# Backward filling products behind the dV/dK products, issued as four 32-column tiles

## The chip, the core and the metric

The kernel runs on one core of a Trainium2 chip. A core has a matrix engine (PE; its weight loads are listed apart as PEld), a vector engine (DVE), an activation engine (ACT), a general engine (POOL) and a sync engine (SP) that issues most transfers. Each takes its own instructions in order, and they wait for one another by semaphores. The metric is the device time of one launch in microseconds (us), as the median of several runs. Before the change it is 1469.26 us (six runs, 1463.87 to 1473.15).

## The reference

A transformer block's forward pass and all its gradients, in bf16, for one sequence of S = 2048 rows of D = 448, H = 16 heads of 28 columns, and a feed-forward width of F = 1792:

```python
def _A_ref(x, wqkv, wo):
    qkv = transpose((x @ wqkv).reshape(B, S, 3, H, Dh), 2, 0, 3, 1, 4)
    q, k, v = qkv[0], qkv[1], qkv[2]
    p = softmax(einsum("bhqd,bhkd->bhqk", q, k) * Dh ** -0.5)
    o = einsum("bhqk,bhkd->bhqd", p, v)
    return transpose(o, 0, 2, 1, 3).reshape(B, S, D) @ wo
...
def _B_ref(x, w_gate, w_up, w_down):
    return (silu(x @ w_gate) * (x @ w_up)) @ w_down
...
xn = layernorm(x)
out = x + _A_ref(xn, wqkv, wo) + _B_ref(xn, w_gate, w_up, w_down)
# returned: out, and the gradients of x, wqkv, wo, w_gate, w_up, w_down for a given grad_out
```

## The kernel before, in words

The first part, up to about 640 us, is the forward attention with the feed-forward layer and its gradients filled in between. The second part is the backward attention, and the change lies there. Its loop goes over `NB` = 512 steps k: 4 groups of heads, 2 halves of a group, 4 chunks of 512 keys, 4 chunks of 512 queries, and 4 tiles of 128 queries. A step handles two heads, each held in 32 partitions or columns (`HP` = 32).

What a step issues is written out by hand, by m = k % 4 (the loop over `range(NB + 12)`):

- Every step begins with `row(k)`: four products with a contraction over 32 rows, two for the scores of step k (line 810, into `sb`) and two for the gradient of the probabilities of step k - 1 (line 818, into `db`). `sb` and `db` have three one-bank PSUM buffers each. They run in the array mode that the profile writes as 32*128: rows by columns of one tile.
- `ew(k)` then gives ACT the two exponentials that read `sb` (line 837) and DVE the two multiplications that read `db` and the exponentials of the step before (line 845).
- `kv` follows for steps whose inputs are due: four products (lines 918 and 922), which add to dV and dK of two heads. Each fills 32 of the 128 output columns of the array, so the four lie side by side: mode 128*32. At m = 1 and m = 2 usually two steps' worth is issued. After each 16 steps the sum is moved out of PSUM by ACT, and the next `kv` waits for m = 3 instead of m = 2.
- At m = 0 stands a transposition of dS (`tr_unit`, line 900, mode 128*128, also into a `db` buffer), at m = 1 the dQ products (`dq_unit`, line 949, 16 in mode 128*32, into the only `genb` bank, which ACT reads out in lines 953 and 962).
- The rest of PE's time goes to filling units, taken from the list `stream`: generators that yield after every product with its estimated duration. `fill_step(room)` runs products until the room is used up. The room is 400 ns (`R0`) before the transposition at m = 0 and without limit behind it, 250 (`R2`) at m = 2, and 750 (`R3`) at m = 3. With products of 189 ns each that is two and then the rest at m = 0, one at m = 2, four at m = 3.

The filling units, all in mode 128*128 (or 128*64 where a chunk has only 64 columns) and all into `genb`: the late columns of the feed-forward weight gradients (`late_dw`, line 884), the gradient of wqkv (`dwq_unit`, line 1014), the forward output (`y_unit`, line 1076), and two parts of the gradient of x (`dx_unit`, line 1132, and `dc_unit`, line 1176). Units of transpositions (`dsq_unit` line 982, `dsp_unit` line 1001) are in the list too; the change does not touch them.

So at m = 2 PE goes through row (32*128), kv (128*32), fill (128*128), and at m = 3 through row (32*128), fill (128*128), with kv in between only in the one case of four named above.

Of the kernel before, what the change touches and what calls it, by code (L numbers as in the profile page):

```python
# [17 lines left out]
D = 448  # L18
# [3 lines left out]
G = 4  # L22
HP = 32
NT = S // 128
NFC = F // 128
P = 128
# [77 lines left out]
def kernel(  # L104
# [23 lines left out]
    PE, DVE, ACTE, POOL, SP = nc.tensor, nc.vector, nc.scalar, nc.gpsimd, nc.sync  # L128
# [18 lines left out]
    xn_sp = xn_t[:, :NT * D].rearrange("p (t d) -> p t d", d=D)  # L147
# [399 lines left out]
    for i in range(len(chain) + LEAD):  # L547
# [4 lines left out]
        k = i - LEAD  # L552
# [115 lines left out]
    for c in range(3):  # L668
        k = 4 * c
        t = 4 * c + 4  # L670
# [99 lines left out]
    def have(*keys):  # L770
        for x in [x for x in slow if x[1] in keys]:
            slow.remove(x)
            SP.dma_start(out=x[2], in_=x[3])
# [19 lines left out]
    def store(o, i):  # L793
        held.append((now + 2, o, i))
        flush(0 if now < NB else 10 ** 9)
# [64 lines left out]
    k = n = 0  # L860
# [14 lines left out]
    fT = bk.tile([P, 4, 2, 4, P], BF16, name="dsp", bufs=1)  # L875
# [3 lines left out]
    def late_dw(c):  # L879
        d0, dn = DCH[c]  # L880
        have(("f",))
        ps = ps_g.tile([P, 2, P], FP32, name="genb")
        for t in range(NT):
            PE.matmul(ps[:dn], lhsT=xn_sp[:, t, d0:d0 + dn], rhs=fT[:, t // 4, :, t % 4, :],
                      start=(t == 0), stop=(t == NT - 1))
            if t < NT - 1:
                yield 110
        DVE.tensor_copy(out=w2[:dn, c], in_=ps[:dn])
        for a, o in enumerate((out_4, out_5)):
            store(o[d0:d0 + dn, F - P:], w2[:dn, c, a])  # L890
        yield 110

    dq_acc = bk.tile([P, S // 2], FP32, name="dq_acc", bufs=1)

    def tr_unit(b):
        ds = dss.pop(4 * b + 3)
        for qi in (3,) if b < NB // 4 - 1 else (2, 3):
            ps = ps_b.tile([P, 8, P], BF16, name="db", bufs=3)
            for c in range(8):
                PE.transpose(ps[:, c, :], ds[:, qi % 2, c // 4, (c % 4) * P:(c % 4 + 1) * P], ident_bf[:])  # L900
            o = dsT[b][:, qi].rearrange("p j kt s -> p (j kt) s")
            if qi == 2:
                DVE.tensor_copy(out=o, in_=ps[:])
            else:
                ACTE.copy(out=o, in_=ps[:])  # L905
# [84 lines left out]
    dsp = {}  # L990
# [19 lines left out]
    def dwq_unit(g, c, tag="genb"):  # L1010
        d0, dn = DCH[c]
        ps = (ps_b if tag == "rest" else ps_g).tile([P, 3 * P], FP32, name=tag, bufs=2 if tag == "rest" else 1)
        for t in range(NT):
            PE.matmul(ps[:dn, :], lhsT=xn_sp[:, t, d0:d0 + dn], rhs=dsp[g][:, t].rearrange("p k r -> p (k r)"),
                      start=(t == 0), stop=(t == NT - 1))
            if t < NT - 1:
                yield 162
        o = bk.tile([P, 3, 4, DH], BF16, name="dwq_o")
        p4 = ps[:].rearrange("p (k h r) -> p k h r", k=3, r=HP)
        cp = ACTE.copy if tag == "rest" else DVE.tensor_copy  # L1020
        cp(out=o[:dn, 0], in_=p4[:dn, 0, :, :DH])
        cp(out=o[:dn, 1:3, 0:2, :], in_=p4[:dn, 1, :, :DH].rearrange("p (k h) r -> p k h r", k=2))
        cp(out=o[:dn, 2, 2:4, :], in_=p4[:dn, 2, 0:2, :DH])
        cp(out=o[:dn, 1, 2:4, :], in_=p4[:dn, 2, 2:4, :DH])
        store(wq_out[d0:d0 + dn, :, g * 4 * DH:(g + 1) * 4 * DH],
              o[:dn].rearrange("p k h r -> p k (h r)"))
        s_done.add((g, c))
        yield 162
# [4 lines left out]
    NH = NFC // 2  # L1033
    ych, yts = {}, {}
# [16 lines left out]
    wd_sb = yp.tile([P, NFC, D], BF16, name="wd_sb", bufs=1)  # L1051
    wo_sb = yp.tile([P, G, D], BF16, name="wo_sb", bufs=1)
# [11 lines left out]
    def y_unit(ch, half, ti):  # L1064
        if ti == 0:
            have(("y", ch, half))
            nxt = 2 * ch + half + 2
            if nxt < 8:
                load_y(nxt // 2, nxt % 2)
        tsl = slice(ti * P, (ti + 1) * P)  # L1070
        mm = [(ych[ch, half][:, i, tsl], wd_sb[:, half * NH + i, :]) for i in range(NH)]
        if half:
            mm += [(ych[ch, 3][:, i, tsl], wo_sb[:, i, :]) for i in range(G)]
        ps = ps_g.tile([P, 512], FP32, name="genb")
        for i, (l, r) in enumerate(mm):
            PE.matmul(ps[:, :D], lhsT=l, rhs=r, start=(i == 0), stop=(i == len(mm) - 1))
            if i < len(mm) - 1:
                yield 189
        if half == 0:
            yts[ti] = yp.tile([P, D], FP32, name="yt", bufs=5)  # L1080
            DVE.tensor_tensor(out=yts[ti][:], in0=ps[:, :D], in1=ych[ch, 2][:, ti, :], op=ALU.add)
        else:
            y = yp.tile([P, D], BF16, name="y")
            DVE.tensor_tensor(out=y[:], in0=ps[:, :D], in1=yts[ti][:], op=ALU.add)  # L1084
            store(out0_d[:, 4 * ch + ti, :], y[:])
        yield 189


    dxs = {}
# [30 lines left out]
    def dx_unit(ch, fq, ti):  # L1120
        if ti == 0:
            have(("dx", ch, fq))
            nxt = 4 * fq + ch + 1
            if nxt < 12:
                load_dx(nxt % 4, nxt // 4)
        d = dxs[ch, fq]
        f0, f1 = FQ[fq]
        n = 2 * (f1 - f0)
        tsl = slice(ti * P, (ti + 1) * P)
        ps = ps_g.tile([P, 512], FP32, name="genb")  # L1130
        for i in range(n):
            PE.matmul(ps[:, :D], lhsT=d[:, i // 2, i % 2, tsl], rhs=dxs["w", fq][:, i // 2, i % 2, :],  # L1132
                      start=(i == 0), stop=(i == n - 1))
            if i < n - 1:
                yield 189
        o = dxs["g"][:, 4 * ch + ti, :]
        if fq == 0:
            ACTE.copy(out=o, in_=ps[:, :D])
        else:
            DVE.tensor_tensor(out=o, in0=ps[:, :D], in1=o, op=ALU.add)  # L1140
        yield 189
# [3 lines left out]
    dcs, dy2 = {}, {}  # L1145
# [23 lines left out]
    def dc_unit(t):  # L1169
        if t % 4 == 0:  # L1170
            have(("dc", t // 4))
            if t < 12:
                load_dc(t // 4 + 1)
        ps = ps_g.tile([P, 512], FP32, name="genb")
        for i in range(3 * G - 3):
            PE.matmul(ps[:, :D], lhsT=dcs[t // 4][:, i, (t % 4) * P:(t % 4 + 1) * P], rhs=dxs["wq"][:, i, :],
                      start=(i == 0), stop=(i == 3 * G - 4))
            if i < 3 * G - 4:
                yield 189
        DVE.tensor_tensor(out=dxs["g"][:, t, :], in0=ps[:, :D], in1=dxs["g"][:, t, :], op=ALU.add)  # L1180
        yield 189
# [14 lines left out]
    for t in range(NT):  # L1196
        stream.append((189 * 9, lambda t=t: dc_unit(t)))
# [25 lines left out]
    def fill_step(room):  # L1223
        nonlocal cur
        if cur is None:
            return
        for ns in cur:
            room -= ns
            if room < ns / 2:
                return  # L1230
        cur = None
# [3 lines left out]
    for k in range(NB + 12):  # L1235
        now = k
        if k < NB:
            g, hp, kc, qc, qi = steps[k]
            if hp == 1 and kc > 0 and qc == 2 and qi == 2 and g + 1 < G:
                load_k(g + 1, kc - 1)  # L1240
            if g > 0 and hp == 0 and kc == 0 and qc == 2 and qi == 2:
                load_k(g, 3)
            if hp == 1 and g + 1 < G and qi == 3 and (kc, qc) in NEXT:
                load_q(g + 1, NEXT.index((kc, qc)))
        m = k % 4
        if k <= NB:
            if k >= K0:
                row(k)
                ew(k)
            flush(k)  # L1250
            if 2 <= k:
                drop()
        if m:
            while kv_n < NB and kv_n <= k - (2 if m == 2 or kv_n % 16 == 15 else 3) and (m != 2 or kv_n % 16):
                kv(kv_n)
                kv_n += 1
        if m == 0:
            b = (k - 8) // 4
            if 9 <= k < NB and cur is None:
                fill_open(600)  # L1260
            fill_step(R0)
            if 0 <= b < NB // 4:
                tr_unit(b)
            fill_step(BIG)
        elif m == 1:
            b = (k - 13) // 4
            if 0 <= b < NB // 4:
                dq_unit(b)
        elif m == 2:
            if 9 <= k < NB:  # L1270
                fill_open(BIG)
                fill_step(R2)
        else:
            fill_step(R3)
    while stream:
        for _ in stream.pop(0)[1]():
            pass
# [14 lines left out]
    g = G - 1  # L1292
# [96 lines left out]
```

The softmax here doesn't subtract the row's maximum and nothing guards it: scores larger than these inputs give would overflow.

## Time and profile before

| | |
|---|---|
| median of six runs | 1469.26 us |
| the profiled execution's own time | 1473.15 us |
| its span, first to last instruction | 1471.4 us |
| mean granted clock of the matrix engine | 0.978 of full speed |
| PE / ACT / DVE busy, of the span | 91% / 86% / 78% |
| matmuls, weight loads | 12647, 12708 |

A row of the profile's list of groups gives the line, the engine, the operation, what it writes and reads, the shapes and the count, then the busy time in us, the mean duration of one in ns, the idle time of the engine just before it, and what ended that idle time. The groups of the backward loop on PE, ACT and DVE that matter here:

```profile
L845 DVE TENSOR_TENSOR ds_sb<-db,e_sb 128x512 bf16<-128x512 f32 x1024 | 648.2, 684 | 72.5 <-PE db L818 25.2
L837 ACT ACTIVATE e_sb<-sb 128x512 bf16<-128x512 f32 x1024 | 554.3, 611 | 60.4 <-PE db L818 43.7
L922 PE MATMUL acc<-ds_sb,qd 128*32 128x512 bf16 x1024 | 162.4, 394 | 0.0
L1132 PE MATMUL genb<-wguT,dau_c 128*128 128x448 bf16 x448 | 117.5, 356 | 6.3 <-ACT dq_st L962 3.8
L949 PE MATMUL genb<-dsT,kd 128*32 128x256 bf16 x2048 | 82.1, 282 | 5.9 <-DVE y L1084 4.3
```

The first says: 1024 multiplications on DVE, 648.2 us in all, 684 ns each; DVE sat idle for 72.5 us before them, 25.2 of which ended with a `db` product of line 818. [...]matmuls which follow one another overlap; how fast they pass is seen in the distance of their starts.

### The profile page before, as it was taken

How to read it: one execution, taken by the hardware profiler on the slowest of the kernel's cores; microseconds unless marked ns; L12 is line 12 of the kernel's file. 1: busy time of each engine (PE TensorE's matmuls, PEld its weight loads, DVE VectorE, ACT ScalarE, POOL GpSimd, SP SyncE). 2: the span in 40 equal slices, each digit the busy share in tenths (PEclk: the TensorE clock that was granted, in tenths of full speed). 3: DMA queues.
4: the chain of work that ended last, by engine and by line, in shares of the span. 5: the costliest groups of instructions: out<-in, count | busy, mean ns of one | idle time of the engine just before them, and what ended most of it. 6: DMA issues, size and time to landing. Idle time of an engine off the chain costs nothing. (4 is left out here: it accounts for less than half of the span.)

```text
span 1471.4 us, 34341 instructions
## 1 busy us (share of the span) xinstructions
PE 1338.5 (91%) x12647; PEld 544.0 (37%) x12708; DVE 1153.4 (78%) x1997; ACT 1263.4 (86%) x2193; POOL 363.3 (25%) x486
## 2 busy tenths in 40 slices
PE   5899999989999999888999989999999999899996
PEld 2333333333333333333333334433343444343343
DVE  6677656756667767487888879888889999899988
ACT  5798888988999988687888879899889899888974
POOL 6465424553344444000001101001001011010005
PEclk9999999999999999999899999999999999999998
DMA  5797957796788675699999999999999999999971
GB/s 150 166 203 194 206 116 183 155 206 154 155 171 190 142 179 139 200 198 194 210 200 201 212 206 189 202 210 209 220 196 187 198 216 201 209 205 199 201 141 59
DMA packets 697665, 271.14 MB, mean 184 GB/s; under 512 B 616129, under 2 KB 672153, under 8 KB 697497
## 3 DMA queue, kind: packets, MB, share of 16 engines
q1 hardware_dynamic: 692520, 262.82, 86.8%
q0 software_dynamic: 3568, 5.83, 1.9%
q8 instruction: 100, 1.64, 0.5%
q14 instruction: 69, 0.56, 0.1%
q10 hardware_dynamic: 1408, 0.30, 0.1%
HBM read 65.04 MB, written 59.90 MB: 85 GB/s over the span
## 5 line engine op out<-in xcount | busy, mean ns | idle before, releaser
L845 DVE TENSOR_TENSOR ds_sb<-db,e_sb 128x512 bf16<-128x512 f32 x1024 | 648.2, 684 | 72.5 <-PE db L818 25.2
L837 ACT ACTIVATE e_sb<-sb 128x512 bf16<-128x512 f32 x1024 | 554.3, 611 | 60.4 <-PE db L818 43.7
L611 ACT ACTIVATE eT<-s_w 128x1024 bf16<-128x1024 f32 x256 | 263.5, 1029 | 48.2 <-PE s_ps L608 45.4
L613 ACT ACTIVATE eT<-s_ps 128x512 bf16<-128x512 f32 x512 | 280.4, 612 | 0.0
L818 PE MATMUL db<-kd,qd 32*128 32x512 bf16 x1024 | 240.4, 386 | 20.6 <-DVE ds_sb L845 19.6
L810 PE MATMUL sb<-kd,qd 32*128 32x512 bf16 x1024 | 212.0, 390 | 8.0 <-DMA qd<-QD_d 4.3
L964 POOL TENSOR_TENSOR dq_acc<-dq_acc,dq_st 128x256 f32<-128x256 f32 x64 | 46.4, 725 | 587.3 <-ACT dq_st L962 587.3
L922 PE MATMUL acc<-ds_sb,qd 128*32 128x512 bf16 x1024 | 162.4, 394 | 0.0
L918 PE MATMUL acc<-e_sb,qd 128*32 128x512 bf16 x1024 | 160.5, 394 | 1.4 <-DVE dw_o L527 1.4
L905 ACT COPY dsT<-db 128x1024 bf16<-128x1024 bf16 x128 | 130.1, 1016 | 35.3 <-PE db L900 34.7
L379 POOL TENSOR_TENSOR nn<-nn,ag 128x512 f32<-128x512 f32 x56 | 71.2, 1271 | 250.7 <-DVE ag L377 242.1
L608 PE MATMUL s_ps<-QQ,KK 32*128 32x512 bf16 x512 | 125.5, 385 | 3.8
L1132 PE MATMUL genb<-wguT,dau_c 128*128 128x448 bf16 x448 | 117.5, 356 | 6.3 <-ACT dq_st L962 3.8
L608 PE MATMUL s_w<-QQ,KK 32*128 32x512 bf16 x512 | 100.3, 387 | 13.1 <-ACT eT L611 10.5
L810 PEld LDWEIGHTS <-qd 32*128 32x128 bf16 x1024 | 48.4, 91 | 152.5 <-issue 140.6
L420 PE MATMUL gen<-xn_t,f_sp 128*128 128x448 bf16 x416 | 91.8, 354 | 2.6 <-DVE nn L394 1.7
L949 PE MATMUL genb<-dsT,kd 128*32 128x256 bf16 x2048 | 82.1, 282 | 5.9 <-DVE y L1084 4.3
L420 PEld LDWEIGHTS <-f_sp 128*128 128x128 bf16 x640 | 55.7, 98 | 76.8 <-issue 31.9
L900 PE MATMUL db<-ident_bf,ds_sb 128*128 128x128 bf16 x1032 | 81.1, 223 | 1.1 <-DVE ds_sb L845 1.1
L900 PEld LDWEIGHTS <-ds_sb 128*128 128x128 bf16 x1032 | 69.5, 100 | 28.5 <-issue 9.7
L380 POOL TENSOR_TENSOR nn<-nn,tt 128x512 f32<-128x512 f32 x56 | 72.0, 1286 | 4.4
L450 PE MATMUL gen<-eT,VS 128*32 128x512 bf16 x1024 | 68.3, 383 | 4.5 <-DVE nn L394 2.4
(163 smaller groups left out, 1871.8 us busy)
## 6 DMA issues: line engine op xcount, KB each, us to landing
F_d<-hda SPq DMA_DIRECT2D x56, 384.0 KB
dau_c<-F_d SPq DMA_DIRECT2D x56, 256.0 KB
h_c<-F_d SPq DMA_DIRECT2D x24, 256.0 KB
qd<-QD_d SPq DMA_DIRECT2D x24, 256.0 KB
dc<-dqkvT_d SPq DMA_DIRECT2D x12, 384.0 KB
dsT<-ds_sb SPq DMA_TRANSPOSE x255
wT_d<-wT_f SPq DMA_DIRECT2D x14, 256.0 KB
KD_d<-qk_sp SPq DMA_DIRECT2D x7, 512.0 KB
```

Source lines behind the costliest of these rows:

```text
L420: PE.matmul(ps[:, :D], lhsT=fsp[fc][:, t // 4, w, t % 4, :], rhs=rhs[:, t, :], start=(t == 0), stop=(t == NT - 1))
L608: PE.matmul(sp4[hh], lhsT=KK[g][r:r + HP, kt * P:(kt + 1) * P], rhs=QQ[g][r:r + HP, qsl], start=True, stop=True, tile_position=(r, 0))
L611: ACTE.activation(out=e2[0][:], in_=wide[:], func=ACT.Exp, scale=SCALE)
L613: ACTE.activation(out=e2[1][:, j], in_=sp4[2 + j], func=ACT.Exp, scale=SCALE)
L810: PE.matmul(s_ps[:], lhsT=qside[g, qc][r:r + HP, 0, qi * P:(qi + 1) * P], rhs=kside[g, kc][r:r + HP, 0, :], start=True, stop=True, tile_po ...
L818: PE.matmul(d_ps[:], lhsT=qside[g, qc][r:r + HP, 1, qi * P:(qi + 1) * P], rhs=kside[g, kc][r:r + HP, 1, :], start=True, stop=True, tile_po ...
L837: ACTE.activation(out=est[k][:, j], in_=sps.pop((k, j))[:], func=ACT.Exp, scale=SCALE)
L845: DVE.tensor_tensor(out=ds[:, qi % 2, j], in0=dps.pop((k - 1, j))[:], in1=est[k - 1][:, j], op=ALU.mult)
L900: PE.transpose(ps[:, c, :], ds[:, qi % 2, c // 4, (c % 4) * P:(c % 4 + 1) * P], ident_bf[:])
L905: ACTE.copy(out=o, in_=ps[:])
L918: PE.matmul(a[r:r + HP, :], lhsT=sp4[:, 1, r:r + HP], rhs=e[:, j, :], start=first, stop=last, tile_position=(0, r), skip_group_check=True)
L922: PE.matmul(a[r:r + HP, :], lhsT=sp4[:, 0, r:r + HP], rhs=ds[:, qi % 2, j, :], start=first, stop=last, tile_position=(0, r), skip_group_ch ...
```

## The change

A helper `mm` takes the place of the direct call in the five kinds of filling products. While the flag `split` is off it issues the same product as before. While it is on, it issues one product for each 32 columns of the stationary operand (four, or two where there are 64), in mode 128*32, each into its own 32 partitions of the same PSUM bank, all over the same moving operand. The flag is set in every step to whether m is 2 or 3, so that the filling products at m = 0 stay whole. A unit may begin split and end whole.

```diff
+    split = False
+
+    def mm(ps, lhsT, rhs, start, stop):
+        if not split:
+            PE.matmul(ps, lhsT=lhsT, rhs=rhs, start=start, stop=stop, skip_group_check=True)
+            return
+        for c in range(0, lhsT.shape[1], HP):
+            PE.matmul(ps[c:c + HP], lhsT=lhsT[:, c:c + HP], rhs=rhs, start=start, stop=stop,
+                      tile_position=(0, c), skip_group_check=True)
...
         for i in range(n):
-            PE.matmul(ps[:, :D], lhsT=d[:, i // 2, i % 2, tsl], rhs=dxs["w", fq][:, i // 2, i % 2, :],
-                      start=(i == 0), stop=(i == n - 1))
+            mm(ps[:, :D], d[:, i // 2, i % 2, tsl], dxs["w", fq][:, i // 2, i % 2, :], i == 0, i == n - 1)
             if i < n - 1:
                 yield 189
...
         m = k % 4
+        split = m > 1
         if k <= NB:
...
+    split = False
     while stream:
```

`late_dw`, `dwq_unit`, `y_unit` and `dc_unit` call `mm` in the same way. In `y_unit` a local list that was named `mm` is now `ops`.

## The prediction

> **What bounds the kernel now.** I read three views, from coarse to fine. First the page's busy shares, and the busy times of most of the backward pass alone (the stretch 660 to 1410 us, where the diff acts; columns: length, then busy us of PE, PEld, DVE, ACT, POOL, granted clock, DMA share, GB/s).
>
> ```profile
> PE 1338.5 (91%) x12647; PEld 544.0 (37%) x12708; DVE 1153.4 (78%) x1997; ACT 1263.4 (86%) x2193; POOL 363.3 (25%) x486
> ...
> 660.00:1410.00 750.00, 698.92 (x7872) 290.69 (x7871) 659.96 (x1101) 661.61 (x1229) 62.79 (x87) 0.98 1.05 202
> ```
>
> In this stretch PE is busy for 93% of the time, but DVE and ACT for 88% each. All three lie close together, so a saving on PE counts only where DVE and ACT wait for PE. Second, the waits of PE, DVE and ACT from 660 to 1420 us (total us, times, longest):
>
> ```profile
> PE db L818 <- DVE ds_sb L845: 18.9, 31, 2.5
> ...
> DVE ds_sb L845 <- PE db L818: 22.9, 54, 1.7
> ...
> ACT e_sb L837 <- PE db L818: 36.8, 113, 2.0
> ```
>
> Each waits for the others; no one engine holds the end. Third, the PE timeline over an ordinary pair of steps, and the first DVE product in it:
>
> ```profile
> 1004.57 0.39 PE L810 MATMUL sb<-kd,qd 32*128 32x512 bf16 x2
> 1004.58 0.39 PE L818 MATMUL db<-kd,qd 32*128 32x512 bf16 x2
> 1004.89 0.39 PE L918 MATMUL acc<-e_sb,qd 128*32 128x512 bf16 x2
> 1004.90 0.39 PE L922 MATMUL acc<-ds_sb,qd 128*32 128x512 bf16 x2
> 1005.12 0.38 PE L918 MATMUL acc<-e_sb,qd 128*32 128x512 bf16 x2
> 1005.13 0.38 PE L922 MATMUL acc<-ds_sb,qd 128*32 128x512 bf16 x2
> 1005.44 0.36 PE L1132 MATMUL genb<-wguT,dau_c 128*128 128x448 bf16 x1
> 1005.74 0.41 PE L810 MATMUL sb<-kd,qd 32*128 32x512 bf16 x2
> 1005.78 0.47 PE L818 MATMUL db<-kd,qd 32*128 32x512 bf16 x2
> 1006.18 0.93 PE L1132 MATMUL genb<-wguT,dau_c 128*128 128x448 bf16 x4
> 1007.04 0.39 PE L810 MATMUL sb<-kd,qd 32*128 32x512 bf16 x2
> ...
> 1005.13 0.69 DVE L845 TENSOR_TENSOR ds_sb<-db,e_sb 128x512 bf16<-128x512 f32 x1 [0.34 <-PE db L818]
> ```
>
> The reader should see two things. Array modes: L918/L922 run as 128*32, the filling product L1132 as 128*128, the row's L810/L818 as 32*128. And the two db products: in the row at 1004.57 both together take 0.39 us, in the row at 1005.74 they take 0.47, so the second started about 0.09 us after the first, at 1005.78 + 0.47 - 0.37 = 1005.88. The DVE product of the row before ended at 1005.13 + 0.69 = 1005.82. db has three buffers, so the second db of this row takes the one that this DVE product read. Record by record: wherever the last db product starts more than 12 ns after the one before it (in 88 of 117 rows with k%4 = 0, 81 of 117 with 1, 31 of 117 with 2, 75 of 117 with 3), it starts 51 to 53 ns after the end of the DVE product that held its buffer. PE comes to these rows early and waits for DVE, too shortly to show as idle time.
>
> **The saving.** From the last of four dV/dK products to the next: in the same mode 207 ns (to the dQ products L949, median of 126; 1004.90 to 1005.12 shows the set's period), to a filling product 311 ns (1005.13 to 1005.44). A mode change costs 104 ns. The first filling product after one takes 10 ns more than its successors (199 against 189). A kv set stands directly before a filling product 112 times: 89 with k%4 = 2, 23 with k%4 = 3. Gross: 112 x 114 ns = 12.8 us.
>
> **The added work.** With k%4 = 2, 128 filling products are split, with k%4 = 3, 478; 30 of these 606 have 64 columns, so that 576 x 3 + 30 = 1758 matmuls and as many weight loads are added (matmuls 12647 to 14405). No shown row is a four-tile product over one shared moving operand; near are kv (448 of its columns would be 189 ns of its 216 ns period for 512) and dQ, four tiles over 256 columns, whose sets start every 109 ns. In full mode 448 columns take 189 ns and 384 take 163, so 2.4 columns pass per ns, and 256 would take 109: a four-tile set streams like one product. The tiles of one set start 3 to 4 ns apart, so that the last stands 10 ns behind the first and the next row comes 10 ns later: after dQ (last tile) and after a fill the row follows 96 ns beyond the stream alike. I take 0 per set, plus 10 ns per stretch. The change into 128*32 after a row is no dearer than that into 128*128 (last db to L918 301 ns, to L1132 303). In m=3 (k%4 = 3) without kv nothing is saved then: row, fill, row changes mode twice before and after. Below nothing a set can't go, since the columns that stream are the same.
>
> **A rule that speaks against this.** The Trainium skill, "TensorE: Matmul & The Clock Gate", Part 3, says that weight loads overlap running matmuls only where their row group differs. Four column tiles share all row groups; by its section "LDWEIGHTS" a load takes columns / 1.2, 27 ns for 32, so four in the open would be an estimated 107 ns a set, 65 us on PE for 606 sets. The row says otherwise: dQ sets with four such loads each follow one another at 109 ns, all stream. "TensorEngine Tiling (Array Packing)", section "Restrictions", adds that column tiling gives up fast weight load; the records give 97 ns for a 128-column load (L1132) and 95 to 100 for a 32-column one (L918, L949). I go by the trace for the sum, and keep 107 ns as the upper end.
>
> **What of it is on the path.** With k%4 = 2 the product that gets 104 ns earlier is followed by a k%4 = 3 row, the one whose second db waits for DVE: its lateness in the steps 7, 11, 15 of 16 is 94, 61 and 93 ns in the median. That DVE product started when the row *before* the fill had delivered its db (DVE waited for PE, 0.34). The chain is row, DVE product, second db of the next row, four filling products; the single fill lies beside it. What PE saves there becomes a longer wait of the db product in line 818. Row by row: 94 ns net (114 less the 10 of the added stretch and 10 for the first product, which has no successor where one fill fits), less the lateness of the following row, never below 0, leaves 3.9 of 112 x 94 = 10.5 us: 2.1 us of 89 cases with k%4 = 2 and 1.9 of 23 with k%4 = 3, where the row after is mostly not late. Less the lateness of the row after that, 1.1 us. I take 2.5, the middle, since a row that comes earlier also lets DVE and ACT start earlier.
>
> Against that stands the 10 ns of each k%4 = 3 stretch. Where the next row is late it costs nothing (0.2 us in all); but its sb products, which ACT waits for at k%4 = 0 rows, start with the row: 112 x 10 = 1.1 us, and 2.2 if skew makes it 20. I take 1.2. The 1758 pairs must be fetched too: the page's instruction queue q8 moved 1.64 MB, and if that is PE's 25355 instructions, 14% more is 0.23 MB beside 271. As for issuing them, PE shows sets of eight instructions every 109 ns (dQ), the new need eight in 189. ACT, DVE, POOL, SP and every transfer keep their instructions and order, and a set signals at its last tile as kv does. No wait is added.
>
> Sum: -2.5 + 1.2 = -1.3 us. The profiled execution took 1473.15 (span 1471.4), so 1471.9 against itself; it lies 3.9 above the median of the six runs, so against the median 1469.26 - 1.3 = 1468.0 us.
>
> **The rivals.** (1) The savings reach the end: if DVE follows PE, 112 x 94 - 1.1 = 9.4 us, 1459.9. For it: PE at 93% and ACT's 36.8 us of waiting for rows. Against: the 51 to 53 ns. (2) Slower: four tiles over one moving operand cost more than one product (reads that collide, or loads in the open). Place: the four sets of a k%4 = 3 step, which lie between DVE's release and the next row. At 50 ns a set, 200 ns a step: with the lateness of the next row taken off, 16 us remain, with that of two rows 7; less 2.5 that is +4.5 to +13.5, 1478 in the middle. At 107 ns, 112 x 0.43 = 48 us less what lateness hides (some 6) gives about 1509. It decides from some 40 ns a set. For it: no row shows a shared operand. Against: dQ's 109 ns. (3) It doesn't do what it says: PE changes mode anyway, since the operands of kv and fill differ. Then only +1.2: 1470.5. Against: kv to dQ, 207 ns.
>
> **How the numbers follow.** Hidden, as worked out: 0.68, its own range 1464 to 1472. Rival 1: 0.12. Rival 2: 0.13. Rival 3: 0.07. 0.5% is 7.3 us and about what a measurement of this kernel can tell from no change. Faster by more comes from rival 1 nearly alone, 0.12; slower by more from rival 2, 0.13; the rest, 0.75. The range takes in the upper ends of the hidden case, its spread (the six runs lie 9 us apart) and the near edge of both other sides: 1461 to 1475.
>
> **What would show it.** In the new trace, kv to fill should be about 207 ns, sets of four fills 189 ns apart, with 14405 matmuls; the second db of k%4 = 3 rows should wait some 90 ns longer, still 52 ns after DVE's end. If sets stand over 200 ns apart, rival 2 holds; if the lateness stays as it was while steps get shorter, rival 1. I would be wrong if DVE's products started earlier than the row before them explains.

## The result and the profile after

The changed kernel takes 1474.59 us in the median of 19 runs, against 1469.46 for the kernel before in the same series: a ratio of 1.0043, interval 1.0030 to 1.0056, by this ratio some 6 us slower. The forecast was 1468.0, slightly faster, with a range of 1461 to 1475; the time lies at the upper edge of the range, and the sign is wrong. The first profiled execution of the changed kernel was a slow one (1494.07 us, outside of the 19), so the profile of a second series of the same kernel (span 1473.3 us, ratio 1.0061) is shown here. The lines have moved: L898 is now a whole filling product, L901 a split one, L927/L931 are dV/dK, L958 is dQ.

The page's busy shares and the stretch 660 to 1410 us, as ahead of the prediction:

```profile
PE 1340.8 (91%) x14387; PEld 555.7 (38%) x14448; DVE 1154.5 (78%) x1997; ACT 1261.9 (86%) x2193; POOL 363.5 (25%) x486
```

```profile
660.00:1410.00 750.00, 697.91 (x9470) 301.26 (x9467) 658.96 (x1099) 660.25 (x1230) 62.64 (x86) 0.97 1.08 202
```

PE has 1740 more matmul records (1758 were forecast; a few records are missing) and is busy for the same 698 us of the stretch. Only the weight loads are busy for longer (301 us in place of 291); no other engine has more work than before. The PE timeline over the same pair of steps, and DVE in it:

```profile
1004.46 0.39 PE L810 MATMUL sb<-kd,qd 32*128 32x512 bf16 x2
1004.47 0.39 PE L818 MATMUL db<-kd,qd 32*128 32x512 bf16 x2
...
1005.01 0.38 PE L927 MATMUL acc<-e_sb,qd 128*32 128x512 bf16 x2
1005.02 0.38 PE L931 MATMUL acc<-ds_sb,qd 128*32 128x512 bf16 x2
1005.23 0.36 PE L901 MATMUL genb<-wguT,dau_c 128*32 128x448 bf16 x4
1005.52 0.51 PE L810 MATMUL sb<-kd,qd 32*128 32x512 bf16 x2
1005.67 0.46 PE L818 MATMUL db<-kd,qd 32*128 32x512 bf16 x2
1006.06 0.94 PE L901 MATMUL genb<-wguT,dau_c 128*32 128x448 bf16 x16
1006.94 0.39 PE L810 MATMUL sb<-kd,qd 32*128 32x512 bf16 x2
```

```profile
1005.02 3.17 DVE L845 TENSOR_TENSOR ds_sb<-db,e_sb 128x512 bf16<-128x512 f32 x5 [0.35 <-PE db L818]
```

Locally the change does what was forecast. From the dV/dK set to the filling product there are 0.21 us (5.02 to 5.23; 0.31 before). The next row comes 1.06 us after the last one (1.17 before). There the saving ends: the first of DVE's five products ends at 1005.71 (records: 0.692 long), and the second db of the row starts at 1005.763, 53 ns after it. The following row stands 1.42 us later (1.30 before), so the pair of steps takes 2.48 us, as before (2.47).

The waits from 660 to 1420 us:

```profile
DVE ds_sb L845 <- PE db L818: 22.3, 52, 2.1
PE db L818 <- DVE ds_sb L845: 17.5, 29, 2.0
DVE ds_sb L845 <- DMA dsT<-ds_sb: 17.1, 13, 2.9
```

The last line was there before as well, and the forecast never looked at it:

```profile
DVE ds_sb L845 <- DMA dsT<-ds_sb: 19.3, 14, 2.5
```

DVE waits for a transfer, the transposition of dS that holds the `ds_sb` buffer.

**Where the time is.** I cut the backward loop of both traces into cycles of 16 steps (start of a row to that of the row 16 later). In about half of the cycles the length repeats to 0.02 us from profile to profile; call these undisturbed. Three of them:

```
cycle from k =           208     240     336
before, and its repeat   24.52   24.52   23.28
changed kernel           24.43   24.43   23.20
```

So the change gains 0.09 us in such a cycle; carried over to all 32 cycles that is an estimated 2.9 us in the forecast's direction (most undisturbed cycles gain this much, a few gain nothing or up to 0.5). The loss is in the other cycles. The clearest is k = 384, 23.8 us before and in its repeat, 27.8 in the changed kernel: this one cycle holds 4 of the some 6 us. SP's timeline there (start, length of the issue), first before, where the cycle starts at 1227.6:

```profile
1228.69 1.25 SPq L826 DMA_TRANSPOSE dsT<-ds_sb  x1
1229.99 1.05 SPq L767 DMA_DIRECT2D dau_c<-F_d  x2
1231.15 3.49 SPq L830 DMA_TRANSPOSE dsT<-ds_sb  x1
1234.68 0.57 SPq L767 DMA_DIRECT2D qd<-QD_d  x1
```

and in the changed kernel, where it starts at 1228.1:

```profile
1232.91 1.25 SPq L826 DMA_TRANSPOSE dsT<-ds_sb  x1
1234.22 1.64 SPq L767 DMA_DIRECT2D dau_c<-F_d  x2
1235.96 3.13 SPq L830 DMA_TRANSPOSE dsT<-ds_sb  x1
1239.13 0.58 SPq L767 DMA_DIRECT2D qd<-QD_d  x1
```

SP issues without a gap in both. But the same first load of qd is issued 7.1 us after the start of the cycle before, and 11.0 after: SP's queue is 3.9 us further behind PE. What that does in this cycle (waits of the changed kernel from 1228.1 to 1255.9, and the stretch of before and of the changed kernel, with the granted clock in the third column from the end):

```profile
DVE ds_sb L845 <- DMA dsT<-ds_sb: 3.0, 2, 2.0
PE db L818 <- DVE ds_sb L845: 2.3, 2, 1.8
```

```profile
1227.60:1251.40 23.80, 22.46 (x271) 10.00 (x271) 22.31 (x36) 22.00 (x42) 2.18 (x3) 1.00 1.04 194
```

```profile
1228.10:1255.90 27.80, 24.18 (x322) 10.61 (x319) 23.72 (x39) 22.10 (x42) 2.18 (x3) 0.94 1.03 216
```

DVE waits for a late transposition, PE for DVE, and the granted clock falls to 0.94 where it was 1.00 before the change: behind these waits the clock record has one stretch of 3.4 us at half speed, from 1238.7. In the kernel before this cycle has no such wait of DVE or PE. Over the whole backward pass such waits prove nothing: two profiles of the unchanged kernel have 27.9 and 16.6 us of PE's and DVE's waits for transfers (620 to 1450 us), that of the changed kernel 26.9. So the causes have to be separated by experiments.

### The profile page after: what moved, and what is told of

The parts are those of the page before. It is cut to its first block, busy times and chain, and to the rows that moved or that the text cites. A ratio compares the mean times of both kernels' runs of the same rounds, so it can differ in the third digit from the quotient of the medians.

```text
span 1492.3 us, 37821 instructions
## 1 busy us (share of the span) xinstructions
PE 1347.4 (90%) x14387; PEld 556.9 (37%) x14448; DVE 1153.2 (77%) x1997; ACT 1262.6 (85%) x2193; POOL 361.9 (24%) x486
## 3 DMA queue, kind: packets, MB, share of 16 engines
q8 instruction: 113, 1.85, 0.5%
## 5 line engine op out<-in xcount | busy, mean ns | idle before, releaser
L818 PE MATMUL db<-kd,qd 32*128 32x512 bf16 x1024 | 248.5, 391 | 20.6 <-DVE ds_sb L845 19.5
L931 PE MATMUL acc<-ds_sb,qd 128*32 128x512 bf16 x1024 | 165.5, 401 | 0.0
L927 PE MATMUL acc<-e_sb,qd 128*32 128x512 bf16 x1024 | 163.5, 401 | 1.3 <-DVE dw_o L527 1.3
L958 PE MATMUL genb<-dsT,kd 128*32 128x256 bf16 x2048 | 82.5, 283 | 10.5 <-DVE y L1092 4.9
L958 PEld LDWEIGHTS <-kd 128*32 128x32 bf16 x2048 | 56.6, 100 | 47.4 <-issue 18.7
```

The costliest lines, as they stand in the source:

```text
L818: PE.matmul(d_ps[:], lhsT=qside[g, qc][r:r + HP, 1, qi * P:(qi + 1) * P], rhs=kside[g, kc][r:r + HP, 1, :], start=True, stop=True, tile_po ...
L927: PE.matmul(a[r:r + HP, :], lhsT=sp4[:, 1, r:r + HP], rhs=e[:, j, :], start=first, stop=last, tile_position=(0, r), skip_group_check=True)
L931: PE.matmul(a[r:r + HP, :], lhsT=sp4[:, 0, r:r + HP], rhs=ds[:, qi % 2, j, :], start=first, stop=last, tile_position=(0, r), skip_group_ch ...
L958: PE.matmul(ps[r:r + HP, :256], lhsT=ks[:, kt, h:h + HP], rhs=t[:, par::2, j, kt, :], start=(kt == 0), stop=(kt == 3), tile_position=(0, r ...
```

## The experiments

Theory A, *queue*: the tiles are free, but the added instructions, or what goes with them, delay SP's transfers. Theory B, *set*: four tiles over one operand cost PE time (the forecast's rival 2). Theory C, *clock*: the granted clock falls by itself. Each ratio is to the kernel before on the same chip.

**The unchanged and the changed kernel again, and one half of the change alone** (`split = m == 2`, `split = m == 3` in place of `m > 1`).

> The kernel before, unchanged, as its own experiment: ratio 1.000 within 0.2%. It gives the granted clock and the span of several runs of it. Clock theory (the change leaves more stretches of 3.4 us at half clock): its mean granted clock lies at 0.976 to 0.978, some 0.004 above that of the changed kernel, and runs of the two kernels with the same clock take the same time within 2 us. Set theory (four tiles cost more than one product where they are on the path): the two kernels have the same clocks, and the changed one is slower by 5 us at every clock.

> The changed kernel again, for a second profile and the clocks of more runs: ratio 1.003 to 1.006 as measured. Clock theory: mean clock about 0.973, and its slower runs are those with the lower clock. Set theory: time above the kernel before by 5 us also where the clock is 0.977.

> Split only where k%4 is 2 (89 of the 112 spared mode changes, 128 of the 606 split products). Set theory: no cost, since single sets lie beside the DVE product: -2 to 0 us. Clock theory: the spared 104 ns become waiting of the matrix engine in the next row, so that most of the loss is here: +3 to +4 us, with a clock about 0.974.

> Split only where k%4 is 3 (23 of the spared mode changes, 478 of the split products). Set theory: all the loss is here, +5 to +7 us, at an unchanged clock. Clock theory: little waiting is added here, 0 to +2 us.

Measured: 1.0007 (0.9991 to 1.0024) for the unchanged, 1.0061 (1.0038 to 1.0084) for the changed kernel; m = 2 alone 1.0017 (0.9998 to 1.0036), m = 3 alone 1.0070 (1.0045 to 1.0094), +10.3 us. So most of the loss comes with the splitting at m = 3; the 2.5 us of m = 2 alone are not told from none. The undisturbed cycles seem to say the opposite: with m = 2 alone 24.52 and 23.28, no gain at all (the saving is hidden, as forecast), with m = 3 alone 24.43 and 23.20, the whole gain of 0.09. The sets of m = 3 stand 189 ns apart, as the whole products did. PE isn't slowed where the splitting takes place, and still the kernel is slower.

**Fewer added instructions at m = 3**: two tiles of 64 columns, and four tiles only where dV/dK were issued in the same step.

```diff
-        for c in range(0, lhsT.shape[1], HP):
+        for c in range(0, lhsT.shape[1], 2 * HP):
...
-        split = m > 1
+        split = m == 3
```

```diff
-        split = m > 1
+        split, kv_0 = False, kv_n
...
         else:
+            split = kv_n > kv_0
             fill_step(R3)
```

> Split only where k%4 is 3, and into two tiles of 64 columns: 450 products more instead of 1372, a third of the added instructions, in a tiled array mode all the same (and no mode change spared). Fetch theory: +2 to +3 us. Set theory: +6 to +8 us, as with four tiles there.

> Split only in those k%4 = 3 steps in which dV/dK products stand directly before the filling ones (23 of the 112): 294 products more, and the only mode changes whose sparing shortened undisturbed cycles, by 0.09 us each 16 steps. Both theories: small. Fetch theory: +1.0 for the instructions less 2 us of spared changes, -1 us. Set theory: a fifth of the loss of k%4 = 3, +1.5 us.

Measured: 1.0014 (1.0001 to 1.0027) and 0.9997 (0.9979 to 1.0014). The first costs 0.06 us in an undisturbed cycle (24.58 and 23.34), an estimated 32 x 0.06 = 1.9 us, nearly all of its 2.1. The second gains 0.10 to 0.11 there, some 3.4 us, and shows 0.4: it is level with the kernel before. With 450 and 294 products added, in place of the 1372 of m = 3 alone, the loss is gone, or nearly.

**More instruction blocks on PE without any split.** PE's instructions arrive in packets of 16 KB on the queue q8; from 660 to 1410 us (packets, MB, share of 16 engines), before and after:

```profile
q8 instruction: 62, 1.02, 0.6%
```

```profile
q8 instruction: 75, 1.23, 0.7%
```

To get more of them without other changes, I filled PE's list in the kernel before to a multiple of 32 or 64 slots after the m = 2 filling.

```diff
                 fill_step(R2)
+                PE.addr_align(32)
```

> The kernel before, whole filling products, with an alignment to 32 instruction slots in the matrix engine's stream after each filling stretch with k%4 = 2: about 28 empty slots 126 times, some 3500 in all, as many as the change adds (3480), and no matrix work. Fetch theory (the change pays for the 13 more 16 KB instruction blocks that the profile's queue q8 shows, which lie among the transfers of a stage whose transfers are nearly saturated): about as slow as the changed kernel, +5 to +6 us, with q8 at 113 packets. Set theory (tiles on the path at k%4 = 3): 0 us. If the empty slots took time on the path by themselves, undisturbed cycles of 16 steps would take longer than the 24.52 and 23.28 us of before.

> The same with an alignment to 64 slots: about 60 empty slots 126 times, some 7500, twice as many as the change adds. Fetch theory: +10 to +13 us, q8 at about 130 packets. Set theory: 0 us.

Measured: 1.0646 (1.0620 to 1.0672) and 1.3129 (1.3102 to 1.3156). Inconclusive: the empty slots cost PE itself 96 and 460 us (the cycle from k = 208 takes 28.2 and 40.0 us in place of 24.5, the second at a clock of 0.87 over the run), which hides any effect of 9 or 21 blocks. The same on POOL, which has idle time:

> The kernel before, with the padding in POOL's stream instead of the matrix engine's: an alignment to 64 slots once in four steps, behind POOL's addition, where POOL has some 5 us of idle time; some 7500 empty slots, which by the run with 28 of them cost at most 60 ns each, 3.6 us. No matrix instruction is added. Fetch theory (an instruction block in flight holds up the transposes beside it: in the traces they land 0.8 to 1.2 us later beside a 16 KB block of the matrix engine, 0.4 us later beside an 8 KB block of the others): about 60 more 8 KB blocks, 60 x 0.4 = 24 us of delay against 13.6 x 1.0 = 14 us for the change, so +8 to +16 us. If only the matrix engine's own instructions matter: 0 us.

> The same with an alignment to 32 slots: about half the blocks. Fetch theory: half of the loss of the 64-slot padding, +3 to +8 us. Otherwise 0 us.

Measured: 1.0009 (0.9995 to 1.0022) and 1.0002 (0.9988 to 1.0017), with 44 and 23 more packets on q14. Those hold 8 KB each and aren't PE's. The expectation of 8 to 16 us for blocks of any engine is thereby refuted.

**What a block does to SP.** In 11 profiles with all loads I took each packet of q8 between 660 and 1400 us with no other instruction packet within 4 us, and summed by how much SP's issues that overlap it exceed the median of their line. It is 629 +- 22 ns for a packet of q8 (459 packets), 39 +- 15 for one of q14 (157, with none of q8 within 4 us), and 5 +- 14 at random times (602). An example of before: a packet is under way from 1001.21 to 1002.36, and

```profile
996.16 0.98 SPq L767 DMA_DIRECT2D wguT<-wT_d  x2
997.23 3.02 SPq L830 DMA_TRANSPOSE dsT<-ds_sb  x1
...
1001.65 1.59 SPq L767 DMA_DIRECT2D wguT<-wT_d  x2
1003.34 3.58 SPq L830 DMA_TRANSPOSE dsT<-ds_sb  x1
```

The issue that overlaps it, two loads of wguT, takes 1.59 us in place of 0.98. (The transposition of 3.58 us starts 1 us after the packet's end and isn't counted with it.) From 660 to 1400 us SP's issues fill 687 of 740 us in the kernel before, 529 of these with transpositions, so that little room is left to make a delay up.

The transfers themselves are held up as well. From issue to landing a transposition takes 3.2 us (one tile) or 4.8 us (two) in the median when no instruction packet is under way, 4.2 or 6.0 beside one of q8, and 3.6 or 5.3 beside one of q14 (seven profiles of the kernels that add 0 to 1758 products).

**How far SP's queue falls behind.** Call the time from the end of the DVE product that completes a transposition's input to its issue the lag of SP. At step 297 it is 0.03 us in every profile: the queue is empty. From there to step 377 it grows, and the cycle from k = 384 follows it:

```
                          q8 packets,       lag at     cycle from
                          steps 297 to 384  step 377   k = 384
before, and its repeat    11, 11            3.4, 2.6   23.8, 23.8
POOL filled, 32 and 64    11, 11            3.6, 4.7   23.8, 25.0
two tiles                 12                2.2        23.8
behind dV/dK alone        12                4.4        23.8
m = 2 alone               12                6.3        26.7
changed                   14                7.1        27.8
m = 3 alone               13                7.9        27.7
cut in three (below)      15                3.3        24.0
```

The time lost goes with the lag in all of them: up to 4.4 us of lag cost nothing, 4.7 cost 1 us, 6 to 8 cost 3 to 4. The lag does not go with the number of packets: the kernel cut in three has the most of them here, and the lag of before.

**Taking the loads away.** If the loss comes through the transfers, it must vanish when they have room. In these kernels the loads of h_c, x_c, o_c, dau_c and dc are left out for all chunks but the first, whose data are used again, so that the first two outputs (the forward result and the gradient of x) aren't the reference's.

```diff
+        if ch:
+            dxs[ch, fq] = dxs[0, fq]
+            return
```

(and the same for `ych` and `dcs`).

> The kernel before with less traffic in the backward pass: of the operands that the filling products read in four chunks (h_c, x_c, o_c, dau_c, dc) only the first chunk is loaded and used for all four, so that three quarters of these loads are left out, and the outputs that depend on them are not those of the reference. Products, order and other transfers stay. Fetch theory: the waits for transposes and the stretches at half clock behind them become fewer, so it is faster than the kernel before by 5 to 15 us. If transfers set nothing: 0 us.

> The changed kernel with the same loads left out, to be set beside the reduced kernel before. Fetch theory: with room on the transfer queues the added blocks cost little and the 0.09 us for each 16 steps that the change saves in undisturbed cycles remain, so 0 to 3 us faster than the reduced kernel before. If the added instructions cost matrix-engine time by themselves: 6 to 9 us slower, as with all loads.

Measured: 0.9867 (0.9842 to 0.9892) and 0.9846 (0.9820 to 0.9872), 1450.13 and 1448.21 us. That is 20 us faster than with all loads, more than the 5 to 15 expected. SP's issues now take 607 of 740 us in the first, and the lag at step 377 is 0.4 and 1.2 us. With the loads the change costs 6 us, without them it shows a gain of 1.9, near the 2.9 of the undisturbed cycles. The intervals of these two ratios are some 3.7 us wide to either side, so the gain is hardly told from none, but it lies apart from a loss of 6. The cycle k = 384 of the changed kernel with fewer loads is an undisturbed one, at full clock:

```profile
1205.70:1229.50 23.80, 22.46 (x322) 10.25 (x319) 22.98 (x38) 21.98 (x42) 2.19 (x3) 1.00 1.09 213
```

A packet of q8 still holds up a transposition's landing here, by 0.9 us (one tile) and 0.8 us (two), and with room that costs nothing. But leaving out loads relieves the 16 DMA engines along with SP: from 660 to 1410 us they move 176 GB/s in place of 202, and their busy share falls from 1.05 to 0.95. Whether SP's queue or the engines behind it set the loss is not separated by these runs.

**More PE instructions of another kind.** Each filling product, at every m, is cut into three along its moving columns (150, 150, 148; `late_dw` into two), in the whole-array mode. The sums of these products aren't the reference's, so this kernel serves for its time alone.

```diff
+        for c in cuts:
+            PE.matmul(ps[c], lhsT=lhsT, rhs=rhs[c], start=start, stop=stop, skip_group_check=True)
```

> The kernel before with every filling product of the backward pass cut along its moving columns into three (150, 150 and the rest; the products of late_dw into two), in whole-array mode, at all k%4: 2192 products more, 17 more instruction blocks of 16 KB, no tiled mode, no mode change spared or added, each moving column read once as before. Block theory (each block of the matrix engine's stream holds up SP's queue by 0.64 us; that queue is issuing for 93% of the stage): 17 x 0.64 = 11 us of queue time, of which about half or more reaches the end, +5 to +11 us. Tile theory (four tiles reading one operand disturb the transfers, or tiled mode costs by itself): only the matrix time of 2 x 2.5 ns a product, +1 to +2 us.

Measured: 1.0068 (1.0053 to 1.0083), +10.0 us, with no filling product in four tiles. The granted clock is 0.976 in the mean of its runs, against 0.975 before: a clock that falls isn't needed for such a loss. But the undisturbed cycles are longer too, 24.68 and 23.44, so PE's own cost is an estimated 32 x 0.155 = 5.0 us (1 to 2 were expected), and only the other 5 would come from 18 blocks. To separate the two, the same with fewer loads, and m = 3 alone likewise:

> The three-column-group kernel with the loads of the later chunks left out, as in the two kernels with fewer loads (the first two outputs aren't the reference's). With all loads the cutting cost 10.0 us (1.0068), of which the undisturbed cycles of 16 steps, +0.155 us each, explain 32 x 0.155 = 5.0 us as PE time of the cut itself; the other 5 us would be the 17 more instruction blocks. Queue theory: with the loads gone SP has room, so only PE's own 5 us stays: 1450.1 + 5 = about 1455, ratio to the kernel before about 0.990. If the cut costs its 10 us on PE wherever the loads are (no part of it through the transfers): 1460, ratio 0.9935.

> Split at k%4 = 3 alone, which with all loads cost +10.3 us (1.007), with the loads of the later chunks left out (the first two outputs aren't the reference's). Queue theory: the loss comes only together with the loads, and what is left is the gain of the undisturbed cycles, -0.09 x 32 = -2.9 us: about 1447, ratio 0.984 to 0.985 against 0.9867 for the same loads without the split. Set theory (the four tiles cost PE time themselves): about 1460, ratio 0.9937.

Measured: 0.9900 (0.9881 to 0.9920), 1455.14 us, and 0.9847 (0.9827 to 0.9867), 1446.63 us: both on the queue theory's numbers. The cut product loses half of its cost with the loads, m = 3 alone all of it:

```
                  cost with all loads   with fewer loads   q8 packets more (page)
changed           +6.3 us               -1.9               13
m = 3 alone       +10.3                 -2.9               10
cut in three      +10.0                 +4.9               18
```

(ratio less 1, or less 0.9867 for fewer loads, times 1469.3; for the changed kernel 1448.21 - 1450.13.)

**Giving SP room in another way.** POOL issues the planned loads in SP's place, in the kernel before, the changed kernel and the one that splits behind dV/dK alone.

```diff
-            SP.dma_start(out=o, in_=i)
+            POOL.dma_start(out=o, in_=i)
```

> The kernel before with the dripped loads of the backward pass (line 767, and those fetched at need) issued by POOL instead of SP; same bytes. SP's issuing falls from about 687 to 580 us of the 740. Block theory: the waits for late transposes go, -3 to -12 us, unless POOL's own issuing costs more. If SP's queue sets nothing: 0 us.

> The changed kernel with the same loads on POOL. Block theory: with room on SP's queue the change no longer costs: 0 to 3 us below the kernel before with loads on POOL. Tile theory: 6 to 9 us above it.

> Loads on POOL, and filling products split only where dV/dK products stand directly before them at k%4 = 3 (294 products more). Block theory: 3 us below the kernel before with loads on POOL, the fastest of all; tile theory: within 1 us of it.

Measured: 1.0267 (1.0221 to 1.0314), 1.0396 (1.0348 to 1.0443) and 1.0333 (1.0305 to 1.0360). Missed: all three are much slower. In the profile of the second SP's issues still take 679 of 740 us, since its transpositions take longer (median of L830 3.45 us, 3.13 in the changed kernel); a single issue of a load on POOL waits up to 29.6 us for PE to free its buffer; and DVE waits 49.8 us for transpositions (620 to 1450 us), up to 11.3 at once, in place of 17.1. Which of these costs the time is not shown. How the change does with an emptier queue and all loads stays untried in a sound form, and no version tried beats the kernel before.

## Why the prediction was wrong

- **The saving, 104 ns a mode change, hidden**: right. dV/dK to fill is 205 ns in the median with k%4 = 2 (207 forecast), and in the pair of steps shown the second db still starts 53 ns after DVE's end. In steps 11 and 15 of 16 it now stands 159 and 184 ns behind the first in the median, in place of 61 and 93: the 90 ns more of waiting that were forecast (step 7 stays at 94). The share that reaches the end was put at 2.5 us less 1.2, a gain of 1.3; the undisturbed cycles give an estimated 2.9 and the kernels with fewer loads 1.9. In the undisturbed cycles it comes wholly from m = 3, where 1.9 of a gross 4.0 us was expected, and not from m = 2.
- **Four tiles cost nothing**: right. Sets stand 189 ns apart, so the upper end of 107 ns a set, and rival 2, which gave the slower side, fall. The sign came out as rival 2 had it, for another reason. That the time still lies inside the range is luck: the range was drawn wide for other reasons.
- **What failed** is the sentence "The 1758 pairs must be fetched too: the page's instruction queue q8 moved 1.64 MB, and if that is PE's 25355 instructions, 14% more is 0.23 MB beside 271", and the price of zero that it stands for, with "ACT, DVE, POOL, SP and every transfer keep their instructions and order". The bytes were right (1.85 MB), and beside 271 MB they are nothing. But the price isn't paid in bytes. A packet of q8 goes with 0.63 us more of SP's issues and about 1 us more to a transposition's landing, and SP's queue, whose fill was never looked up, is 93% full. The order of the transfers stayed; their times didn't: the lag of SP at step 377 is 7.1 us in place of 3.4 and 2.6, DVE waits for the late transposition, and the loss of 6.3 us turns into -1.9 where the transfers have room. The Trainium skill, "Runtime: NRT & Kernel Launch", section "Instruction fetch mechanics", has the 16 KB blocks too and calls the cost of crossing from one to the next "mostly hidden". In the undisturbed cycles it is (24.43 us with the added blocks, 24.52 without); beside it the runs show the longer issues and later landings on SP's queue.
- **How far this is shown.** Shown: the loss of the changed kernel and of m = 3 alone exists only with the loads; in undisturbed cycles PE loses nothing of its own; the largest single loss, k = 384, follows the lag of SP's queue; SP's issues take longer beside PE's blocks, and hardly beside those of q14. Not shown: that the added blocks are what makes the queue lag, and by how much. The sum 13 x 0.63 = 8.2 us of delay less the 2.9 gained gives +5.3 and comes near the 6.3, but by luck: the same sum gives 10 x 0.63 - 2.9 = +3.4 for m = 3 alone (10.3 measured) and 18 x 0.63 + 5.0 = +16.3 for the cut product (10.0). What goes away with the loads is some 8 us for 13 blocks, 13 for 10 and 5 for 18. It may matter where a block falls among the transpositions, and shorter cycles leave SP less time, longer ones more; neither was tested. The experiment that would add blocks and nothing else failed with its empty slots.
- **Clock.** In the mean of all fast runs the granted clock is 0.972 with the change (27 runs) and 0.975 before (119). If every cycle that is not granted counted, 0.003 of 1470 us would be an estimated 4 us; by the spread of the runs (3 to 7 us for 0.01) it is 1 to 2. With fewer loads it is 0.979 in both. That it follows the waits fits k = 384, where the half-speed stretch comes after them, and is not tested by itself.

## What to carry to other kernels

Before adding instructions to one engine "for free", add up how long the issuing engine of the transfers is busy with its issues (here 93%): if it is nearly full, a small delay there can cost time although every compute engine's working is right. Compare cycles of the loop with one another: undisturbed ones gave the gain to 0.01 us, and only the others held the loss. And a cost that vanishes when an unrelated load is left out comes through the transfers, not from the time that the changed instruction itself takes.

## What was not expected of the hardware

- An issue of a transposition keeps SP for 1.25 us (one query tile) or 3.05 us (two), and 0.57 us go to a plain load of 256 KB; 237 transpositions take 529 of 740 us.
- A 16 KB packet of PE's instructions is under way for about 1.1 us and goes with 0.63 us more of SP's issues; the 8 KB packets of q14 take about 0.4 us and go with 0.04. A transposition beside the former lands about 1 us later, beside the latter about 0.5 us later.
- Four column tiles over one shared moving operand follow one another at the pace of one whole product, 189 ns for 448 columns, also at half the clock (373 ns for both).
- Empty slots in PE's instruction list are not free: filling it to multiples of 32 or 64 slots 126 times, 9 and 21 packets more, cost 96 and 460 us.
